# Log-decays summed by two f16 products instead of one f32 product, from the eleventh attention tile on

## The chip, the cores and the metric

The kernel runs on one core of a Trainium2 chip. The time is that of one launch in device microseconds (us). Below, PE is the matrix engine (TensorE), with PEld its loads of stationary operands; DVE is the vector engine, ACT the scalar engine, POOL the GpSimd engine; SP issues the transfers (DMA).

## The reference

A gated linear attention over 4 batches, 8 heads, 768 steps and 48 features a head is followed by a two-layer network over 3072 tokens and by a network of eight experts of 384 tokens each. What the change touches is the attention's decay:

```python
f = 1.0 / (1.0 + np.exp(-f_logit))
for t in range(S):
    state = f[:, :, t, :, None] * state + np.einsum('bhd,bhe->bhde', k[:, :, t], v[:, :, t])
    y[:, :, t] = np.einsum('bhd,bhde->bhe', q[:, :, t], state)
x = np.maximum(0.01 * (x @ w_in), x @ w_in) @ w_out     # then the experts: relu(x @ w1[e]) @ w2[e]
```

## The kernel before

The attention is cut into 24 tiles, numbered 0 to 23: 128 steps of one batch, all eight heads. Inside a tile the decay between two steps is a difference of running sums of log f. So each tile begins with these sums (`s0`, line 394): ACT forms exp(-f_logit) in place in `fT` (three buffers), then log(1 + that) into `ld` (two buffers, 64 columns a head, of which 48 hold data and 16 stay zero); PE multiplies `ld` by `span`, a 128x128 matrix of 0, 1 and -1, one f32 product for each of the four pairs of heads, into the PSUM tile `P`. One f32 product stands in the trace as two weight loads and two matmuls.

`s1` takes the exponentials of P and -P on ACT (`ek`, `eq`, and `dn` for the next state) and multiplies them onto k and q on DVE (`ks`, `qs`), and decays the state (`de`, `St`). `s2` transposes `ks` (`kT`, `kp`). `s3` forms the products A of `ks` and `qs`, which DVE masks (`am`); from tile 8 on `am` is split into high and low f16 halves (`ahl`, ACT and DVE). `s4` forms the output `y` and the state's update `U`; `ys` is y in two f16 halves, which `s5` turns with a transposing DMA into `xT`.

The two-layer network runs on PE beside the attention, three tiles of tokens at a time (a group). Its operands are f16 halves too: `hp` (first layer, 16 blocks a group, three PSUM buffers) is turned by ACT and DVE into `g`, and `g` is split into `gh` (ACT) and `gl` (DVE, in some early blocks POOL); `xp` is the second layer. The weights of both layers arrive as pairs of 32-bit words and are put together by DVE integer operations (`winu`, `woutu`), then split (`winh`, `winl`, `wo`). DVE does this up to the last `wo`, which the first `xp` reads in order of its index f, 0 to 15. After that the experts' weights are loaded (`xw_s`), split (`xw_h` on ACT, `xw_l` on DVE) and stored; `pg` are small products for the later routing, on operands that a transposing DMA delivers (`turned`).

The order of the instructions on each engine is set when the program is built: the first tiles by hand (`START`), the rest by a scheduler, which interleaves the attention's steps with the network's products. Nearly all instructions are recorded by one helper, so they bear the line 84.

Of the kernel before, what the change touches and what calls it, by code (L numbers as in the profile page):

```python
# [10 lines left out]
F16 = mybir.dt.float16  # L11
# [3 lines left out]
AF = mybir.ActivationFunctionType  # L15
OP = mybir.AluOpType
# [2 lines left out]


SQ, SV = 64.0, 64.0
SX, SWI, SG, SWO = 2.0 ** 10, 2.0 ** 7, 2.0 ** 10, 2.0 ** 8
SWG = 2.0 ** 12
SX2, SW1, SW2 = 2.0 ** 6, 2.0 ** 8, 2.0 ** 8
# [67 lines left out]
def body(tc, qk, v, f_logit, w_in, w_out, w_gate, w1, w2, out):  # L92
    nc = tc.nc
    w_in, w_out = w_in.bitcast(I32), w_out.bitcast(I32)
    PE, DVE, ACT, POOL, SP = (InOrder(tc, e) for e in (nc.tensor, nc.vector, nc.scalar, nc.gpsimd, nc.sync))
    InOrder.on = True
    B, CH, _, D, _, NP, _ = qk.shape
    H, S = 2 * NP, 128 * CH
# [9 lines left out]
    NWD = 0  # L108
    NWARM, WU = 0, 4
    MP = (1,)  # L110
    LEAD, PACE0, W0, POOLN, GLN, FT, KP, PB = 3, 1300.0, 1000.0, 8, 2, 8, 4, 3

    with ExitStack() as ctx:
        consts = ctx.enter_context(tc.tile_pool(name="consts", bufs=1))
# [15 lines left out]
        def mm(o, l, r, start, stop):  # L130
            return PE.matmul(o, l, r, start=start, stop=stop, skip_group_check=True)

        def copy(o, i, scale=1.0):
            return ACT.activation(o, i, AF.Copy, bias=0.0, scale=scale)
# [82 lines left out]
        one = consts.tile([128, 1], F32)  # L217
# [11 lines left out]
        dnext = [[apool.tile([128, NP], F32, name=f"dn{b}_{i}") for i in range(2)] for b in range(B)]  # L229
# [7 lines left out]
        span = consts.tile([128, 128], F32)  # L237
# [3 lines left out]
        DVE.tensor_scalar(early, late, -1.0, None, op0=OP.add)  # L241
        DVE.tensor_scalar(span[:, :MID + 1], jp[:, :MID + 1], 0.0, early, op0=OP.is_le, op1=OP.mult)
        DVE.tensor_scalar(span[:, MID + 1:], jp[:, MID + 1:], 0.0, late, op0=OP.is_ge, op1=OP.mult)
        identf = consts.tile([128, 128], F32)
        DVE.tensor_scalar(identf, jp, 0.0, None, op0=OP.is_equal)
        identh = consts.tile([128, 128], F16)
# [147 lines left out]
        def s0(n):  # L394


            t, u = XT["f", n], ld[n % 2]
            ACT.activation(t, t, AF.Exp, bias=0.0, scale=-1.0)
            ACT.activation(u[:, :, :D], t, AF.Ln, bias=one, scale=1.0)
            yield  # L400
            P = banks[0].tile([128, NP, 128], F32, name="P", tag="at", bufs=5)
            for p in range(NP):
                mm(P[:, p, :], u[:, 2 * p:2 * p + 2, :], span, True, True)
            st.setdefault(n, {})["P"] = P


# [12 lines left out]
        def s1(n):  # L419

            c, b = tiles[n]
            P = st[n].pop("P")
            ek, eq = edec[0][n % 2], edec[1][n % 2]
            qs = aw.tile([128, NP, 128], F32, name="qs")
            ks = aw.tile([128, NP, 128], F32, name="ks")
            for t, sign in ((ek, 1.0), (eq, -1.0)):
                ACT.activation(t[:, :, :MID + 1], P[:, :, :MID + 1], AF.Exp, bias=0.0, scale=sign)
                ACT.activation(t[:, :, MID + 2:129], P[:, :, MID + 1:], AF.Exp, bias=0.0, scale=sign)
            if c + 1 < CH:
                ACT.activation(dnext[b][c % 2], P[:, :, 127], AF.Exp, bias=0.0, scale=-1.0)  # L430
            yield
            (POOL if n < KP else DVE).tensor_tensor(ks, XT["qk", n][:, 1], ek[:, :, 1:129], op=OP.mult)
            DVE.scalar_tensor_tensor(qs, XT["qk", n][:, 0], SQ, eq[:, :, 1:129], op0=OP.mult, op1=OP.mult)
            st[n].update(qs=qs, ks=ks)
            if c > 0:
                de = aw.tile([128, NP], F32, name="de")
                DVE.tensor_tensor(de, dnext[b][(c - 1) % 2], ek[:, :, 0], op=OP.mult)
                DVE.tensor_tensor(St[b], St[b], de[:, :, None].to_broadcast([128, NP, 2 * D]), op=OP.mult)
# [631 lines left out]
        n = 0  # L1070
# [12 lines left out]

        live, complete = {}, set()
        names = dict(f=s0, v=s0v, p=s1, k=s2, a=s3, y=s4, x=s5, w=split_win)

        def group_x(n):
# [242 lines left out]
```

## Time and profile before

| | |
|---|---|
| time, median of 3 runs | 785.66 us (784.7 to 787.34) |
| the profiled execution | 781.42 us, of which the span of its instructions is 779.6 us |
| mean granted clock of TensorE | 0.983 of 2.4 GHz |
| PE busy | 94% of the span |
| DVE busy | 72% of the span, 99% of it between 40 and 156 us |
| products P of tiles 10 to 23 | start at 118.51 to 358.98 us |

The profiled execution lies 4.2 us under the median of the three runs, so rows of the trace are summed against 781.42 us, and the difference is carried over to the median. Busy time on PE is modelled at the ends of matmuls, which overlap in the pipeline: how long a group of products holds PE is read from the starts of what stands before and behind it.

### The profile page before, as it was taken

Reading aid. Unit: us, or ns where it says so; the run is one execution under the profiler, and the core shown is the slowest. Engines: PE = TensorE matmul, PEld = TensorE weight load, DVE = VectorE, ACT = ScalarE, POOL = GpSimd, SP = SyncE. Lnnn points to the kernel's source line nnn. Section 1 sums busy time; section 2 is a strip of 40 time slices with the busy share of each in tenths; the row PEclk is TensorE's granted clock in tenths of the full one; section 3 lists DMA queues with packets and bytes.
Section 4 is the critical chain, followed back from the end, with each engine's and each line's share of the span. In section 5 each row is a group of like instructions: output and inputs, shape, how many; then the busy total and the mean of one; then the engine's idle time right before and its main releaser. Section 6 shows DMA issues by size and latency. Waiting matters only on the chain.

```text
span 779.6 us, 15455 instructions
## 1 busy us (share of the span) xinstructions
PE 730.7 (94%) x5900; PEld 484.1 (62%) x5900; DVE 558.8 (72%) x1579; ACT 350.0 (45%) x732; POOL 142.7 (18%) x158
## 2 busy tenths in 40 slices
PE   6888998999999999998999999999989899999995
PEld 5756775677576577676666666555545455556663
DVE  5899999968966967966873958677685676873320
ACT  6566656557755754753663743000123123222320
POOL 5355312000000000000000001010243434535111
PEclk9899899999999999999999999999999999999998
DMA  9965544698897798998898500050475557665300
GB/s 258 249 162 164 161 133 125 152 276 219 237 249 213 210 309 191 250 249 221 238 272 230 166 2 2 23 192 22 148 224 155 177 158 168 228 198 174 107 31 30
DMA packets 111643, 135.90 MB, mean 174 GB/s; under 512 B 62929, under 2 KB 94674, under 8 KB 109522
## 3 DMA queue, kind: packets, MB, share of 16 engines
q1 hardware_dynamic: 106194, 100.31, 49.1%
q0 software_dynamic: 5376, 34.61, 13.1%
q8 instruction: 46, 0.75, 0.4%
q14 instruction: 27, 0.22, 0.1%
HBM read 86.52 MB, written 34.60 MB: 155 GB/s over the span
## 4 chain that ended last, share of the span: by engine, by line
PE 49%; DVE 25%; DMA 9%; issue 8%; ACT 5%; SPq 1%; POOL 1%; another core or an unknown queue 1%; POOLq 0%; ACTq 0%; DVEq 0%
PE hp L84 17%; PE xp L84 17%; PE yp L84 5%; DVE g L84 3%; PE y L84 3%; DVE winu L84 3%; DMA xw_s<-in_moe_w 3%; DMA fT<-in_f_logit 2%; DVE gl L84 2%; DVE woutu L84 2%; DMA turned<-x 2%; DVE xw_l L84 1%; PE P L84 1%; PE U L84 1%; PE c L84 1%
## 5 line engine op out<-in xcount | busy, mean ns | idle before, releaser
L84 PE MATMUL hp<-xT,winh 128*128 128x384 f16 x768 | 191.4, 329 | 11.8 <-DVE g L84 11.7
L84 PE MATMUL xp<-wo,gh 128*128 128x384 f16 x768 | 190.4, 326 | 0.8 <-DVE wo L84 0.8
L84 PE MATMUL hp<-xT,winl 128*128 128x384 f16 x384 | 126.3, 329 | 0.0
L84 PE MATMUL xp<-wo,gl 128*128 128x384 f16 x384 | 125.0, 326 | 0.0
L84 PEld LDWEIGHTS <-gh 128*128 128x128 f16 x912 | 83.9, 97 | 42.6
L84 PEld LDWEIGHTS <-winh 128*128 128x128 f16 x768 | 74.3, 99 | 57.3 <-issue 16.5
L84 PE MATMUL hp<-x2T,w1e 128*128 128x384 f16 x576 | 99.3, 325 | 0.7 <-ACT x2T L84 0.4
L84 PE MATMUL yp<-w2e,hh 128*128 128x384 f16 x384 | 94.4, 325 | 0.0
L84 ACT ACTIVATE g<-hp 128x384 f32<-128x384 f32 x152 | 73.0, 485 | 23.1 <-PE hp L84 21.5
L84 DVE SCALAR_TENSOR_TENSOR g<-hp,g 128x384 f32<-128x384 f32 x128 | 69.5, 552 | 8.2 <-ACT g L84 7.8
L84 PEld LDWEIGHTS <-w1e 128*128 128x128 f16 x576 | 52.3, 97 | 32.9 <-issue 1.1
L84 PEld LDWEIGHTS <-gl 128*128 128x128 f16 x528 | 48.7, 97 | 28.6 <-DVE gl L84 0.9
L84 ACT ACTIVATE gh<-g 128x768 f16<-128x768 f32 x64 | 53.9, 841 | 26.1 <-DVE g L84 25.4
L84 ACT ACTIVATE xw_h<-xw_s 128x768 f16<-128x768 f32 x64 | 53.2, 839 | 25.5 <-DMA xw_s<-in_moe_w 24.7
L84 POOL IOTA jp<- 128x128 f32 x2 | 0.5, 238 | 341.8 <-PE hp L84 341.7
L84 PE MATMUL yp<-w2e,hl 128*128 128x384 f16 x192 | 62.5, 325 | 0.0
L84 DVE TENSOR_TENSOR gl<-g,gh 128x768 f16<-128x768 f32 x52 | 49.7, 956 | 16.8 <-ACT gh L84 16.2
L84 DVE SCALAR_TENSOR_TENSOR xw_l<-xw_s,xw_h 128x768 f16<-128x768 f32 x64 | 60.2, 951 | 1.9 <-ACT xw_h L84 1.9
L84 ACT ACTIVATE hh<-hp 128x384 f16<-128x384 f32 x64 | 31.4, 491 | 62.2 <-PE hp L84 52.1
L84 ACT ACTIVATE x<-yp 128x384 f32<-128x384 f32 x24 | 11.8, 491 | 93.3 <-PE yp L84 75.1
L84 ACT ACTIVATE x<-xp 128x384 f16<-128x384 f32 x24 | 11.7, 489 | 92.0 <-PE xp L84 80.8
L84 PEld LDWEIGHTS <-winl 128*128 128x128 f16 x384 | 37.8, 98 | 22.9 <-issue 0.9
(265 smaller groups left out, 1228.3 us busy)
## 6 DMA issues: line engine op xcount, KB each, us to landing
xw_s<-in_moe_w SPq DMA_DIRECT2D x64, 384.0 KB, 4.0
qkT<-in_qk SPq DMA_DIRECT2D x48, 192.0 KB, 4.1
wout_s<-in_moe_w_out SPq DMA_DIRECT2D x16, 384.0 KB, 3.5
w1d<-xw_h SPq DMA_DIRECT2D x32, 192.0 KB, 4.2
w1d<-xw_l SPq DMA_DIRECT2D x32, 192.0 KB, 4.0
w2d<-xw_h SPq DMA_DIRECT2D x32, 192.0 KB, 4.3
w2d<-xw_l SPq DMA_DIRECT2D x32, 192.0 KB, 4.0
fT<-in_f_logit SPq DMA_DIRECT2D x24, 192.0 KB, 3.5
```

The lines of the kernel that those rows point to most:

```text
L84: i = f(*args, **kwargs)
```

## The change

For tiles 0 to 9 nothing changes. From tile 10 on (`HT`), ACT writes the logarithm in place in f32, ACT copies it, scaled by 2^9, as f16 into the first half of the same `ld` buffer, and DVE writes the rest (the scaled value minus that copy) as f16 into the second half. PE sums both halves in PSUM: two f16 products by `spanh`, an f16 copy of `span`, for each pair of heads. The exponentials take the scale out again. The zero columns of the two buffers are cleared once more, in tiles 10 and 11.

```diff
+        spanh = consts.tile([128, 128], F16)
+        DVE.tensor_copy(spanh, span)
...
             ACT.activation(t, t, AF.Exp, bias=0.0, scale=-1.0)
-            ACT.activation(u[:, :, :D], t, AF.Ln, bias=one, scale=1.0)
+            if n < HT:
+                ACT.activation(u[:, :, :D], t, AF.Ln, bias=one, scale=1.0)
+            else:
+                u = u.rearrange("p h d -> p (h d)").bitcast(F16).rearrange("p (s h d) -> p s h d", s=2, h=H)
+                if n < HT + 2:
+                    DVE.memset(u[:, :, :, D:], 0.0)
+                ACT.activation(t, t, AF.Ln, bias=one, scale=1.0)
+                copy(u[:, 0, :, :D], t, SLD)
+                DVE.scalar_tensor_tensor(u[:, 1, :, :D], t, SLD, u[:, 0, :, :D], op0=OP.mult, op1=OP.subtract)
...
-                mm(P[:, p, :], u[:, 2 * p:2 * p + 2, :], span, True, True)
+                if n < HT:
+                    mm(P[:, p, :], u[:, 2 * p:2 * p + 2, :], span, True, True)
+                else:
+                    for i in range(2):
+                        mm(P[:, p, :], u[:, i, 2 * p:2 * p + 2, :], spanh, i == 0, i == 1)
...
-            for t, sign in ((ek, 1.0), (eq, -1.0)):
+            a = 1.0 if n < HT else 1.0 / SLD
+            for t, sign in ((ek, a), (eq, -a)):
```

The scheduler also places other instructions anew. Three places matter here. The first is DVE where it prepares the last `wo` blocks (about 121 to 128 us of the trace); `g` is the evicted first layer. Before:

```order
L84 TENSOR_SCALAR woutu<-wout_s 128x384
L84 SCALAR_TENSOR_TENSOR g_1305<-hp,g_1305 128x384
L84 SCALAR_TENSOR_TENSOR woutu<-wout_s,woutu 128x384 x2
L84 TENSOR_TENSOR de<-dn_1_126,ek_109 128x4
L84 SCALAR_TENSOR_TENSOR woutu<-wout_s,woutu 128x384
L84 TENSOR_TENSOR am<-A,mask 128x512 x2
L84 SCALAR_TENSOR_TENSOR wo<-woutu,wo 128x384
L84 SCALAR_TENSOR_TENSOR g_1305<-hp,g_1305 128x384
```

The same place on DVE after the change (the first and the second `g` row are the same two blocks, under new numbers):

```order
L85 SCALAR_TENSOR_TENSOR woutu<-wout_s,woutu 128x384 x2
L85 SCALAR_TENSOR_TENSOR g_1307<-hp,g_1307 128x384
L85 SCALAR_TENSOR_TENSOR woutu<-wout_s,woutu 128x384 x2
L85 TENSOR_SCALAR woutu<-wout_s 128x384
L85 TENSOR_TENSOR am<-A,mask 128x512 x2
L85 SCALAR_TENSOR_TENSOR wo<-woutu,wo 128x384
L85 SCALAR_TENSOR_TENSOR g_1307<-hp,g_1307 128x384
```

Counted from the program's start to the second `g` row, one `wo`, two `woutu` and one `de` now stand behind it, and one `memset` and one low half (both tile 10's, some rows earlier) ahead of it.

The second place is PE at P of tile 12, beside the first tile of the second layer (`xp`). Before:

```order
L84 MATMUL xp<-wo,gh 128x384
L84 LDWEIGHTS gh
L84 MATMUL xp<-wo,gh 128x384
L84 MATMUL P<-span,ld_105 128x128 x4
L84 MATMUL A<-qs,ks 128x128 x8
L84 LDWEIGHTS gl
L84 MATMUL xp<-wo,gl 128x384
```

The same place on PE after the change, where six more P rows, an `xp` row among them and the last two A follow the last row shown:

```order
L85 MATMUL P<-spanh,ld_105 128x128
L85 LDWEIGHTS gh
L85 MATMUL xp<-wo,gh 128x384
L85 LDWEIGHTS gl
L85 MATMUL xp<-wo,gl 128x384
L85 MATMUL A<-qs,ks 128x128 x5
L85 LDWEIGHTS gh
L85 MATMUL xp<-wo,gh 128x384
L85 MATMUL A<-qs,ks 128x128
L85 LDWEIGHTS ld_105
L85 MATMUL P<-spanh,ld_105 128x128
```

The high half's first product now goes ahead, and the rest, which needs the low half, stands behind six of A's products; the low half of block f = 15 is read only behind 26 other products of `xp`.

The third place is DVE at about 194 to 200 us, as it stands in the ten or so tiles that follow. Before:

```order
L84 SCALAR_TENSOR_TENSOR g_2264<-hp,g_2264 128x384
L84 SCALAR_TENSOR_TENSOR xw_l<-xw_s,xw_h 128x768
L84 TENSOR_TENSOR de<-dn_0_127,ek_110 128x4
L84 TENSOR_TENSOR St_120<-St_120,de 128x384
L84 TENSOR_TENSOR am<-A,mask 128x512 x2
L84 SCALAR_TENSOR_TENSOR g_2264<-hp,g_2264 128x384
L84 TENSOR_TENSOR ahl<-am,ahl 128x512 x2
L84 TENSOR_TENSOR gl<-g_2264,gh 128x768
L84 SCALAR_TENSOR_TENSOR g_2326<-hp,g_2326 128x384 x2
L84 SCALAR_TENSOR_TENSOR xw_l<-xw_s,xw_h 128x768
```

The same place on DVE after the change:

```order
L85 SCALAR_TENSOR_TENSOR g_2298<-hp,g_2298 128x384
L85 SCALAR_TENSOR_TENSOR xw_l<-xw_s,xw_h 128x768
L85 TENSOR_TENSOR de<-dn_0_127,ek_110 128x4
L85 SCALAR_TENSOR_TENSOR ld_106<-fT_104,ld_106 128x8x48
L85 TENSOR_TENSOR am<-A,mask 128x512 x2
L85 SCALAR_TENSOR_TENSOR g_2298<-hp,g_2298 128x384
L85 TENSOR_TENSOR ahl<-am,ahl 128x512 x2
L85 TENSOR_TENSOR gl<-g_2298,gh 128x768
L85 SCALAR_TENSOR_TENSOR g_2366<-hp,g_2366 128x384 x2
L85 SCALAR_TENSOR_TENSOR xw_l<-xw_s,xw_h 128x768
L85 TENSOR_TENSOR St_120<-St_120,de 128x384
```

The low half takes the place of the state's decay (`St`), which moves behind the next `xw_l`.

## Rows read from the trace of the kernel before

**Rows 1.** Windows: busy us of PE, PEld, DVE, ACT, POOL, clock, DMA share.
```profile
108.00:156.00 48.00, 43.98 (x356) 31.63 (x356) 47.42 (x93) 28.65 (x63) 5.71 (x3) 0.96 0.52 136
156.00:360.00 204.00, 199.70 (x1731) 139.53 (x1728) 154.25 (x277) 124.86 (x251) 0.00 (x0) 1.00 0.91 240
```
**Rows 2.** Waits of DVE, 40 to 156 us: total us, times, longest.
```profile
DVE g L84 <- ACT g L84: 0.2, 1, 0.2
```
**Rows 3.** Waits of PE, 108 to 156 us.
```profile
PE hp L84 <- DVE g L84: 3.4, 3, 2.1
PE xp L84 <- DVE wo L84: 0.8, 2, 0.6
```
**Rows 4.** Waits of PE, 156 to 360 us.
```profile
PE hp L84 <- DVE g L84: 2.6, 4, 0.9
PE pg L84 <- DMA turned<-wo: 1.6, 1, 1.6
```
**Rows 5.** Timeline of PE about P of tile 13: start, us, merged count.
```profile
161.07 1.05 PE L84 MATMUL P<-span,ld 128*128 128x128 f32 x8
162.06 1.16 PE L84 MATMUL A<-qs,ks 64*128 64x128 f32 x16
```
**Rows 6.** Timeline of PE, f16 products of P's size late in the program.
```profile
557.26 0.78 PE L84 MATMUL xT<-identh,xg 128*128 128x128 f16 x11
```
**Rows 7.** Timeline of PE, from an f16 product to A.
```profile
405.61 0.33 PE L84 MATMUL xp<-wo,gh 128*128 128x384 f16 x1
405.86 1.16 PE L84 MATMUL A<-qs,ks 64*128 64x128 f32 x16
```
**Rows 8.** Tile views (`ld`, `xT`): ns min/median/max, first and last start.
```profile
L84 PE MATMUL P<-span,ld x192: 271/275/582, 5.3 to 359.8; 128*128 128x128 f32 x192
...
L84 DVE MEMSET ld<- x2: 165/165/165, 3.4 to 3.5; 128x128 f32 x2
...
L84 PE MATMUL xT<-identh,xg x54: 216/219/230, 557.3 to 736.3; 128*128 128x128 f16 x54
```
**Rows 9.** Groups by form: busy us, mean ns, idle before.
```profile
L84 DVE SCALAR_TENSOR_TENSOR vl<-ld_v,vh 128x384 f16<-128x384 f32 x16 | 8.8, 549 | 0.0
...
L84 ACT ACTIVATE vh<-ld_v 128x384 f16<-128x384 f32 x16 | 8.4, 522 | 0.0
L84 PEld LDWEIGHTS <-xg 128*128 128x128 f16 x54 | 3.3, 98 | 1.3 <-DMA xg<-x2d,row 1.0
```
**Rows 10.** Timeline of DVE: four operations in a row; the state's decay.
```profile
139.34 1.96 DVE L84 SCALAR_TENSOR_TENSOR woutu<-wout_s,woutu 128x384 int32<-128x384 int32 x4
...
151.11 0.55 DVE L84 TENSOR_TENSOR St<-St,de 128x384 f32<-128x384 f32 x1
```
**Rows 11.** Timeline, DVE and PE: the longest wait of PE after 108 us.
```profile
127.04 0.56 DVE L84 SCALAR_TENSOR_TENSOR g<-hp,g 128x384 f32<-128x384 f32 x1
...
127.65 0.48 PE L84 MATMUL hp<-xT,winh 128*128 128x384 f16 x2 [2.14 <-DVE g L84]
...
130.20 0.84 PE L84 MATMUL hp<-xT,winh 128*128 128x384 f16 x2
```
**Rows 12.** Timeline, DVE and PE: the last `wo` and its reader.
```profile
150.10 0.55 DVE L84 SCALAR_TENSOR_TENSOR wo<-woutu,wo 128x384 f16<-128x384 f32 x1
...
150.74 0.49 PE L84 MATMUL xp<-wo,gh 128*128 128x384 f16 x2
```
**Rows 13.** Timeline of PE: P of tile 15 and a wait behind it.
```profile
190.59 1.05 PE L84 MATMUL P<-span,ld 128*128 128x128 f32 x8
...
199.60 0.48 PE L84 MATMUL hp<-xT,winh 128*128 128x384 f16 x2 [0.92 <-DVE g L84]
```
**Rows 14.** Timeline of PE: P of tile 23 and the wait behind it.
```profile
358.98 1.05 PE L84 MATMUL P<-span,ld 128*128 128x128 f32 x8
...
367.37 0.30 PE L84 MATMUL pg<-wgs,turned 128*128 128x16 f16 x6 [0.47 <-DMA turned<-wo]
```

More of the change, by code (lines that the diff above doesn't have):

```diff
@@ L21 @@
 SQ, SV = 64.0, 64.0
+SLD = 2.0 ** 9
 SX, SWI, SG, SWO = 2.0 ** 10, 2.0 ** 7, 2.0 ** 10, 2.0 ** 8
@@ L110, in body @@
     MP = (1,)
-    LEAD, PACE0, W0, POOLN, GLN, FT, KP, PB = 3, 1300.0, 1000.0, 8, 2, 8, 4, 3
+    LEAD, PACE0, W0, POOLN, GLN, FT, KP, PB, HT = 3, 1300.0, 1000.0, 8, 2, 8, 4, 3, 10
     with ExitStack() as ctx:
@@ L429, in s1 @@
             if c + 1 < CH:
-                ACT.activation(dnext[b][c % 2], P[:, :, 127], AF.Exp, bias=0.0, scale=-1.0)
+                ACT.activation(dnext[b][c % 2], P[:, :, 127], AF.Exp, bias=0.0, scale=-a)
             yield
```

## The prediction

> **What bounds the kernel now.** I read the busy time by windows first, then who waits for whom in each window, then single places. The windows [rows 1] split the stretch in which tiles 10 to 23 form their sums into two stages. From 108 to 156 us DVE is busy 47.42 of 48.00 us. In the view of DVE's waits [rows 2] only 0.2 us stand in front of it between 40 and 156 us: DVE is full, and PE, which waits 3.4 us for `g` and 0.8 us for `wo` there [rows 3], follows it. From 156 to 360 us it is the other way round: PE is busy 199.70 of 204.00 us and DVE 154.25, and PE's waits for DVE come to 2.6 us [rows 4]. So a microsecond taken off PE is worth a microsecond in the second stage, and in the first a microsecond put on DVE costs one. Tiles 10, 11 and 12 lie in the first stage, tiles 13 to 23 in the second.
>
> **PE, removed and added.** P of tile 13 starts at 161.07 and A behind it at 162.06 [rows 5]: the four f32 products hold PE for 0.99 us. Inside, eight matmuls start (1.05 - 0.275)/7 = 0.111 us apart (0.275 is how long one lasts [rows 8], 1.05 the row's length); the last is followed by A only 0.99 - 0.775 = 0.215 later, some 0.10 more than the spacing. After the change there are eight f16 products of 128 columns, each with weights of its own. The nearest rows are the f16 products `xT`, of the same size and with new weights nearly each time: eleven in 0.78 us [rows 6], one of 0.219 [rows 8], so (0.78 - 0.219)/10 = 0.056 apart. The step into A costs something too: an `xp` product of the usual 0.16 us is followed by A after 405.86 - 405.61 = 0.25 [rows 7], 0.09 more. I take 7 x 0.056 + 0.056 + 0.09 = 0.54 us, so a saving of 0.99 - 0.54 = 0.45 us a tile; with a step of 0.215 it is 0.38, with none 0.54. Those are the bounds.
>
> **DVE, added.** One low half a tile: the same operation on the same size as `vl`, 0.549 us [rows 9]. Back to back such operations overlap: four in 1.96 us [rows 10] are (1.96 - 0.55)/3 = 0.47 apart. I take 0.47, with 0.55 as the bound. Two clearings, of 0.165 each by the like one at the start [rows 8]. The f16 copy of `span` comes once, at the very start, where DVE next waits for PE and ACT to deliver the first tile; nothing, and at most the 0.55 of one of DVE's usual operations.
>
> **ACT, added.** One f16 copy a tile, 0.522 us like `vh` [rows 9]. ACT is busy 124.86 of 204 us in the second stage [rows 1], and eleven copies add 5.7. The copy stands ahead of `ek` in most tiles, so `ks` and `qs` come half a microsecond later; the A that reads them stands a tile behind, and the network's products between cover it; without that cover it would be 0.5 us a tile. Nothing. The input buffer `fT` is now let go by DVE's low half, so its next load starts up to about 1 us later (a copy and a low half); loads run two tiles ahead, which covers that too.
>
> **The first stage, up to about 156 us.** By the order, the second `g` row of the first place loses a `wo`, two `woutu` and a `de` ahead of it (3 x 0.47 + 0.1 = 1.5 us) and gains a clearing and a low half (0.165 + 0.47 = 0.64). PE waits 2.14 us for exactly this row at 127.65 [rows 11]; the wait should shrink by about 0.9. But the work is only put off. Up to the last `wo`, and to the first `xw_l` behind it, DVE does two clearings and four low halves more (2 x 0.165 + 4 x 0.47 = 2.2 us), less a `de` and an `St` that move behind (about 0.6, from the 0.55 of rows 10): 1.6 us later if DVE stays full. PE stood directly behind DVE there: the last `wo` ends at 150.65, its reader starts at 150.74 [rows 12]. In the new order PE has 26 other products of `xp` (26 x 0.16 = 4.2 us) to do ahead of that reader, and three cheaper P (3 x 0.45 = 1.35 us). Tile 12's P, though, waits in its middle for a low half that DVE reaches only after `ys`: a stall of 0 to 1.7 us. These pull both ways; I take the stage as unchanged, with -1.5 and +1.6 us as ends.
>
> **The second stage.** Eleven tiles save 0.45 us each on PE: 4.95. Three of them give nothing, since PE runs into a wait behind them anyway: tile 15's (190.59), with the wait of 0.92 us for `g` at 199.60 [rows 13], tile 18's, which repeats that pattern, and tile 23's (358.98), ahead of the wait for a transposed operand at 367.37 [rows 14]. Eight are left: 8 x 0.45 = 3.6. DVE's added low halves cost nothing while DVE has 50 us of slack in 204; in the tight place (third place of the order) the low half takes the room of an `St` that moves behind, so `g` isn't later. The sum is -3.6 us: 781.42 - 3.6 = 777.8 for an execution like the profiled one, and 785.66 - 3.6 = **782.1** for the median, which lies 4.2 us higher. That is 0.46% faster; 0.3%, some 2.4 us, is about what a measurement here can tell from no change.
>
> **The rivals.**
> *More than forecast.* The first stage shrinks as well. The stretch behind the wait of 2.14 us runs at half the clock: two products of `hp` last 0.84 us at 130.20 where they take 0.48 at 127.65 [rows 11], that is, 1.2 instead of 2.4 GHz, after PE had stood still. With a shorter wait the drop may not come; the granted clock of the stage, 0.96 over 48 us [rows 1], makes it worth (1 - 0.96) x 48 = 1.9 us. 3.6 + 1.5 + 1.9 = 7.0: 778.7. Against it: clearings and low halves keep DVE full, and the wait shrinks by less than half.
> *Nothing gained in sum.* DVE's 1.6 us go through in full and tile 12's stall with them: -3.6 + 1.6 = -2.0, 783.7. For it: DVE has no idle time there at all.
> *The weight loads show.* A load of 128 f16 columns lasts 0.098 us [rows 9]; if it is not hidden behind the product ahead, the eight are 0.098 apart: 7 x 0.098 + 0.19 = 0.88, a saving of 0.11, 8 x 0.11 = 0.9 us, 784.8. The 0.056 of rows 6 speaks against it, there with the same loads. The Trainium skill ("TensorE: Matmul & The Clock Gate", Back-to-back issue gap) gives about 81 ns for each product of 128 columns in a stream of weight loads and products; by it the saving would be 0.99 - (8 x 0.081 + 0.09) = 0.25 a tile, 2.0 in sum, 783.7. This case's row, 0.056, disagrees, and I go by the row.
> *Slower.* DVE becomes the bound in the second stage too: each low half lies on the path. A tile in which it does costs 0.47 us and saves nothing, any other saves 0.45; from six of the eleven on the gain is gone, and with nine it is 9 x 0.47 - 2 x 0.45 = +3.3, 789.0. For it: the four waits for `g`, all where ACT and DVE split the first layer. Against it: DVE's share there rises only to (154.25 + 11 x 0.47)/200 = 80%.
>
> **How the numbers follow.** Forecast (782.1; by the bounds 780.3, with 0.54 in ten tiles, to 782.6, with 0.38 in eight) 0.46; more than forecast 0.15; nothing gained in sum 0.18; the weight loads show 0.04; slower 0.17. The first two are faster by over 0.3%: 0.61. The next two lie within it: 0.22. The last is 0.17. The range is 778.5 to 787.0: it holds all cases but the far half of the first rival and most of the last.
>
> **What would show it.** Right: between P of tiles 13 and later and the A behind them 0.50 to 0.60 us instead of 0.99; PE's waits for `g` from 156 to 360 us near 2.6 to 4; A of tile 22 some 3.5 to 4 us earlier than before; a first `xw_l` between 155 and 158 us. Wrong: products further apart than 0.08; waits for `g` grown by several microseconds in the second stage; PE standing over 2 us in the middle of tile 12's P; a longer stretch at half the clock after 125 us. It would also be wrong if a gain at 360 us were given back to the transposes of the weights that `pg` waits for.

## The result: 0.6% slower, and the profile after

| | before | after |
|---|---|---|
| median of 22 runs each | 784.88 us (779.21 to 791.04) | 789.88 us (785.15 to 794.48) |
| ratio, 95% interval | | 1.0061 (1.0034 to 1.0089) |
| profiled execution; span | 781.42; 779.6 us | 794.37; 792.6 us |

The forecast was 782.1 us and faster; the time lies above the range too. In this ratio and in those below, executions more than 1.5% above the fastest of their kernel are left out (none of the changed kernel's here, two of nine in load_first). The two profiled executions stand 13 us apart because one is among the fastest of its kernel and the other among the slowest. 3.7 us of that lie in the first 66 us, where the work is the same but for the f16 copy of `span` (the ninth `g` row of DVE ends at 66.32 and 70.00 us); in a further profile of the kernel before that row ends at 69.68. So the spans of two profiles can't be compared here. Stretches can, as far as the same kernel repeats them.

The windows of [rows 1], in the changed kernel:

```profile
108.00:156.00 48.00, 42.01 (x343) 30.38 (x339) 46.09 (x91) 28.40 (x63) 5.43 (x3) 0.93 0.50 130
156.00:360.00 204.00, 195.92 (x1698) 133.68 (x1697) 160.44 (x289) 129.77 (x265) 0.00 (x0) 1.00 0.89 238
```

DVE is still nearly full in the first window and has 44 us of slack in the second, and PE is busy 96% of the second where it was 98%. What PE waited for in the second window, with ACT's and DVE's waits that stand behind it (compare [rows 4]):

```profile
ACT fT L85 <- DMA fT<-in_f_logit: 10.3, 6, 4.0
DVE x L85 <- ACT x L85: 8.8, 5, 4.3
PE hp L85 <- DVE g L85: 6.0, 6, 1.8
```

The longest of these waits are one event. The timeline of the changed kernel there, ACT first, then DVE, then PE (in brackets the idle time ahead of the row and who ended it):

```profile
184.82 0.52 ACT L85 ACTIVATE fT<-fT 128x384 f32<-128x384 f32 x1 [4.05 <-DMA fT<-in_f_logit]
185.25 0.47 ACT L85 ACTIVATE x<-xp 128x384 f16<-128x384 f32 x1
...
185.75 0.56 DVE L85 SCALAR_TENSOR_TENSOR x<-xp,x 128x384 f16<-128x384 f32 x1 [4.33 <-ACT x L85]
...
186.37 0.48 PE L85 MATMUL hp<-xT,winh 128*128 128x384 f16 x2 [0.67 <-DVE x L85]
...
189.74 0.48 PE L85 MATMUL hp<-xT,winh 128*128 128x384 f16 x2 [1.75 <-DVE g L85]
...
195.65 0.52 ACT L85 ACTIVATE fT<-fT 128x384 f32<-128x384 f32 x1 [2.30 <-DMA fT<-in_f_logit]
...
196.71 1.02 PE L85 MATMUL U<-ld_v,kp 128*112 128x96 f32 x8 [1.07 <-ACT kp L85]
```

ACT stands for 4.05 us in front of the exponential of tile 16, whose input has not landed. Behind it on ACT wait the evictions of `x` and of three blocks of `g`, though tile 16's P comes only at 228.13 us; PE, short of PSUM buffers, waits for them. A second stand follows, of 2.30 us in front of tile 17's exponential; `kp` is queued behind it, and PE waits 1.07 us for that. From P of tile 14 to P of tile 15 it takes 18.65 us instead of 14.83. The Trainium skill says the same of the queue ("PSUM — Partial Sum Buffer", Engine vs sequencer instructions: the queues of ScalarE, VectorE and GpSimdE are strictly first in, first out), and the trace agrees: x begins at 185.25, as the exponential ends.

Why the input is late, SP's rows for the loads of `fT` of tiles 13 and 16, before:

```profile
93.19 0.39 SPq L84 DMA_DIRECT2D fT<-in_f_logit  x1
...
142.39 0.35 SPq L84 DMA_DIRECT2D fT<-in_f_logit  x1
```

and after, with what stands just ahead of the second:

```profile
113.39 0.33 SPq L85 DMA_DIRECT2D fT<-in_f_logit  x1
...
172.78 0.34 SPq L85 DMA_DIRECT2D x2d<-x  x1
173.17 2.39 SPq L85 DMA_TRANSPOSE turned<-x  x1
...
179.06 0.44 SPq L85 DMA_DIRECT2D ld_v<-in_v  x1
179.59 0.44 SPq L85 DMA_DIRECT2D w1d<-xw_h  x1
180.09 0.43 SPq L85 DMA_DIRECT2D fT<-in_f_logit  x1
```

The load for tile 13 was issued 25 us ahead of tile 10's P and is now issued 11 us ahead of it, because its buffer is let go by a low half that DVE reaches 20.6 us after ACT's copy (112.81 and 92.18). For tile 16 the buffer is free at 163.3 us, but the scheduler, which reckons with the later release, has put the load behind tile 10's transposes, a `turned` operand and stores of expert weights.

In the first window (compare [rows 3, 11, 12]) PE's waits are, in the changed kernel:

```profile
PE xp L85 <- ACT wo L85: 2.9, 1, 2.9
PE hp L85 <- DVE g L85: 2.7, 3, 2.0
```

The wait of 2.14 us for `g` at 127.65 us is gone (the 0.48 at 133.14 is for the next block). But a new one, of 2.03 us and for a block five earlier, stands ahead of tile 10's P, and later on PE stands 2.94 us for a `wo`; about the end of that stand its clock is halved. The timeline of PE, after:

```profile
118.04 0.48 PE L85 MATMUL hp<-xT,winh 128*128 128x384 f16 x2 [2.03 <-DVE g L85]
...
148.77 0.48 PE L85 MATMUL xp<-wo,gh 128*128 128x384 f16 x1 [2.94 <-ACT wo L85]
...
150.59 0.53 PE L85 MATMUL xp<-wo,gh 128*128 128x384 f16 x1
150.91 0.53 PE L85 MATMUL xp<-wo,gl 128*128 128x384 f16 x1
...
153.34 0.53 PE L85 MATMUL xp<-wo,gh 128*128 128x384 f16 x1
153.66 0.53 PE L85 MATMUL xp<-wo,gl 128*128 128x384 f16 x1
```

The window around it (the columns of [rows 1]):

```profile
147.00:156.00 9.00, 7.23 (x56) 5.92 (x55) 7.29 (x18) 2.85 (x6) 0.00 (x0) 0.62 0.24 69
```

Products of `xp` start 0.32 us apart there, and 0.16 at 167 us, that is, at 1.2 instead of 2.4 GHz. The granted clock of 0.62 in 9 us is a loss of (1 - 0.62) x 9 = 3.4 us. The kernel before has its half-clock stretch from 128.9 to 132.3 us, 3.4 us long, which costs 1.7 by the same reckoning. Both are PE's loss, and an upper bound of the kernel's.

What the change was to save did arrive. P and A of tile 13, after (compare [rows 5]):

```profile
167.88 0.61 PE L85 MATMUL P<-spanh,ld 128*128 128x128 f16 x8
168.41 1.16 PE L85 MATMUL A<-qs,ks 64*128 64x128 f32 x16
```

0.53 us instead of 0.99. Where a tile runs from P to P without a wait, it takes 14.24 instead of 14.68 us.

### The profile page after: what moved, and what is told of

It reads as the page before. It is cut to its first block, busy times and chain, and to the rows that moved or that the text cites. A ratio compares the mean times of both kernels' runs of the same rounds, so it can differ in the third digit from the quotient of the medians.

```text
span 792.6 us, 15484 instructions
## 1 busy us (share of the span) xinstructions
PE 737.2 (93%) x5900; PEld 485.3 (61%) x5900; DVE 564.9 (71%) x1596; ACT 355.7 (45%) x746; POOL 141.7 (18%) x158
## 4 chain that ended last, share of the span: by engine, by line
PE 59%; DVE 22%; issue 7%; DMA 5%; ACT 4%; POOL 1%; SPq 0%; another core or an unknown queue 0%; POOLq 0%; ACTq 0%; DVEq 0%
PE hp L85 20%; PE xp L85 19%; PE yp L85 6%; PE y L85 4%; DVE g L85 3%; DMA fT<-in_f_logit 3%; PE A L85 3%; DVE winu L85 2%; PE P L85 2%; DVE woutu L85 2%; PE U L85 2%; DVE gl L85 1%; PE c L85 1%; DMA turned<-x 1%; ACT gh L85 1%
## 5 line engine op out<-in xcount | busy, mean ns | idle before, releaser
L85 PE MATMUL hp<-x2T,w1e 128*128 128x384 f16 x576 | 100.9, 329 | 0.7 <-ACT x2T L85 0.6
```

The source lines that it names most:

```text
L85: i = f(*args, **kwargs)
```

## The experiments

The first theory was that the late loads of `fT` cost the time (**late load**), the rival that DVE's added work does, in the stage in which DVE is full (**DVE's work**). Each kernel was timed beside the kernel before on the same chip. The medians of the kernel before on these chips were 777 to 783 us, so only ratios are compared. Besides, three lengths are taken from each profile, which leave out the spread of the first 95 us. On DVE, (a) is from the end of the 17th `g` row to that of the 4th `x` row, about 95 to 221 us of the span; (b) from there to the 15th `x`, about 221 to 425 us; (c) from P of tile 14 to P of tile 15, a part of (a). Each is the length in one profiled execution; the two profiles of the kernel before differ by 0.3 us in (a) and 1.0 in (b), those of the changed kernel by 0.1 and 3.9. P of tiles 10 to 16 lies in (a), P of tiles 17 to 23 in (b).

| kernel | ratio | 95% interval | (a) us | (b) us | (c) us |
|---|---|---|---|---|---|
| before (profile at hand) | | | 126.03 | 203.64 | 14.83 |
| before_again | 1.0000 | 0.9967 to 1.0032 | 126.34 | 202.61 | 14.83 |
| after (profile at hand) | 1.0061 | 1.0034 to 1.0089 | 132.49 | 202.86 | 18.65 |
| after_again | 1.0079 | 1.0048 to 1.0111 | 132.56 | 198.99 | 19.91 |
| load_first | 1.0037 | 0.9998 to 1.0075 | 128.22 | 200.44 | 14.39 |
| low_first | 0.9980 | 0.9947 to 1.0012 | 129.58 | 199.15 | 15.41 |
| only_10_to_12 | 1.0054 | 1.0023 to 1.0086 | 131.29 | 201.67 | 14.83 |
| low_on_pool | 0.9992 | 0.9961 to 1.0023 | 126.90 | 200.22 | 14.96 |
| from_13 | 0.9997 | 0.9968 to 1.0026 | 126.02 | 200.53 | 14.39 |
| pool_from_13 | 1.0028 | 1.0000 to 1.0057 | 128.55 | 201.79 | 14.71 |
| first_from_13 | 0.9966 | 0.9930 to 1.0002 | 126.49 | 198.28 | 14.39 |
| first_from_13_b | 1.0000 | 0.9966 to 1.0035 | 126.96 | 198.62 | 14.64 |
| f32_copied | 1.0017 | 0.9984 to 1.0049 | 126.19 | 200.58 | 14.83 |
| high_only | 0.9898 | 0.9851 to 0.9944 | 124.34 | 199.29 | 14.38 |

**before_again and after_again** are the two kernels themselves.

> The kernel before, unchanged: its profile on the chip of the other three, and a measure of what a ratio here can tell. Ratio 1.000 within 0.003. The stretch before tile 10's P, which is the same code in all kernels, should come out anywhere from 118 to 125 us, as it did in the profiles so far; from P of tile 13 to P of tile 23 it should take 195 to 198 us.

> The changed kernel, unchanged, beside the variants on one chip. If its loss is in the order of its instructions, all of it comes back: ratio 1.003 to 1.009, tile 14 to 15 18 to 19 us with a wait of ACT for fT of about 4 us, first xw_l 39 to 40 us after P of tile 10. If that wait was an accident of the one profiled execution, it is 0 to 2 us here and the ratio's cause lies elsewhere.

The ratio of 1.000 came with an interval of 0.3% to both sides. The changed kernel lost again what it had lost, with a wait of ACT for `fT` of 4.57 us in the same place: its loss is in the order of its instructions, and most of it in (a), 132.5 against 126.2 us. From P of tile 14 to P of tile 15 it took 19.91 us, more than expected.

**load_first** moves two loads and leaves PE's order as it is.

```diff
-                    SP.dma_start(t, ap(f_logit, ...))
+                    if n in (15, 16):
+                        with tc.high_priority():
+                            SP.dma_start(t, ap(f_logit, ...))
+                    else:
+                        SP.dma_start(t, ap(f_logit, ...))
```

> The changed kernel, with the loads of fT of tiles 15 and 16 given high priority and nothing else: PE's order is word for word that of the changed kernel, SP issues these two loads ahead of other loads, and ACT takes tile 16's exponential and logarithm some 20 us earlier. If the late load is the cause, 3 to 4.5 us less than the changed kernel beside it: ratio to the kernel before 0.999 to 1.003, tile 14 to 15 14.3 to 15 us, waits of PE for g from 156 to 360 us down from 6 to 2 to 4. If DVE's added work up to the first xw_l is the cause, no difference from the changed kernel: 1.004 to 1.008.

Its timeline: ACT takes tile 16's exponential without a wait, and P of tiles 14 and 15 stand 14.39 us apart.

```profile
164.03 0.51 ACT L85 ACTIVATE fT<-fT 128x384 f32<-128x384 f32 x1
...
179.71 0.61 PE L85 MATMUL P<-spanh,ld 128*128 128x128 f16 x8
...
194.10 0.61 PE L85 MATMUL P<-spanh,ld 128*128 128x128 f16 x8
```

PE's waits for `g` from 156 to 360 us fell to 3.3. Beside after_again it gained 1.0079 - 1.0037 = 0.42%, 3.3 us of 783, a little beyond the range in which late load alone would have put the ratio. The two intervals overlap, so the times alone don't show the gain; the profiles do: with the same instructions in the same order on PE, (c) fell by 5.5 us and (a) by 4.3, and 2 us over the kernel before were left. The wait of 2.95 us for `wo` and the half-clock stretch behind it, 6.8 us long, stayed; its 3.4 us less the 1.7 of before would make nearly all of these 2 us. So late load is the larger part, and not all.

**low_first** lets DVE do each low half early, in all fourteen tiles.

```diff
-                copy(u[:, 0, :, :D], t, SLD)
-                DVE.scalar_tensor_tensor(u[:, 1, :, :D], t, SLD, ...)
+                with tc.high_priority():
+                    copy(u[:, 0, :, :D], t, SLD)
+                    DVE.scalar_tensor_tensor(u[:, 1, :, :D], t, SLD, ...)
```

> The copy and the low half are given high priority, so that DVE does each low half soon after its copy and the next load into the same fT buffer starts about as early as before the change; the work is the same. If the late release of fT is the cause (loads of tiles 13 to 16 started a whole tile later, ACT stood 4.05 us in front of one exponential at 184.8 us and let x and g wait), the loss goes: 784.5 to 786, ratio to the kernel before 0.999 to 1.002, no wait of ACT for fT over 2.5 us in 160 to 205 us, and tile 14 to 15 takes about 14.4 us instead of 18.6. If DVE's added work in the first stage is the cause (first xw_l at 39.6 us after P of tile 10 instead of 37.8), nothing changes: 789 to 790, 1.005 to 1.007, or worse, since low halves now go ahead of the work that PE waits for.

The ratio came out where late load wanted it, or below. The profile, of an execution 6 us over the kernel's median, agrees only in part: (c) is down to 15.41 where 14.4 was expected, ACT still stands once for 2.60 us (at 193.19) where late load wanted nothing over 2.5, and 3.4 us over the kernel before are left in (a), with PE's waits for `wo` of 1.44, 0.81 and 2.14 us.

**only_10_to_12** changes the three tiles of the first stage alone.

```diff
-            if n < HT:
+            if not HT <= n < HT + 3:
+                if HT + 3 <= n < HT + 5:
+                    DVE.memset(u[:, :, D:], 0.0)
...
-                if n < HT:
+                if not HT <= n < HT + 3:
...
-            a = 1.0 if n < HT else 1.0 / SLD
+            a = 1.0 if not HT <= n < HT + 3 else 1.0 / SLD
```

> Only tiles 10, 11 and 12 are changed, those in the stage in which DVE is full; two more clearings in tiles 13 and 14 make the zero columns good again. By the order the load of fT of tile 16 stands ahead of the tenth turned output, so ACT should find it in time. DVE's work as a cause of its own: 3 low halves and 4 clearings, 3 x 0.47 + 4 x 0.165 = 2.1 us, and PE's three savings of 0.45 lost behind them: ratio 1.002 to 1.005, and the first layer's block 32 some 2 us later after its block 24 than in the kernel before (63.0 and 63.8 us there). Late load as the only cause: 0.998 to 1.001.

0.54% slower, 5 us more in (a): above what DVE's work was to cost. Block 32 of the first layer comes 69.4 us behind block 24, 5.6 to 6.4 more than in the kernel before, where some 2 were expected. PE's waits from 108 to 170 us:

```profile
PE xp L85 <- ACT wo L85: 5.1, 2, 2.9
```

The place of the second, on ACT's timeline:

```profile
162.14 0.52 ACT L85 ACTIVATE fT<-fT 128x384 f32<-128x384 f32 x1 [2.12 <-DMA fT<-in_f_logit]
162.57 0.51 ACT L85 ACTIVATE wo<-woutu 128x384 f16<-128x384 f32 x1
```

The first wait for `wo` is that of the changed kernel, with the halved clock behind it. The second is late load once more, and for tile 16 again, though the expectation had ACT find that input in time: ACT stands in front of the exponential, and the last `wo` is queued behind it. Its half-clock stretches, 147.0 to 153.8 and 164.1 to 167.5 us, cost (6.8 + 3.4)/2 = 5.1 us, 3.4 more than that of before, and with the 2.1 us of the second wait that is about what (a) lost. So this run doesn't part the two causes cleanly; it shows that a late load costs most where something else is queued behind it on ACT, and that the three tiles of the full stage alone can lose as much as the whole change does.

**from_13, low_on_pool, high_only** each take the low halves away from DVE in the full stage: by starting later (`HT` 13 instead of 10), by giving them to POOL, or by leaving them out.

```diff
 low_on_pool
-                DVE.scalar_tensor_tensor(u[:, 1, :, :D], t, SLD, ...)
+                copy(t, t, SLD)
+                POOL.tensor_tensor(u[:, 1, :, :D], t, u[:, 0, :, :D], op=OP.subtract)
 high_only
-                DVE.scalar_tensor_tensor(u[:, 1, :, :D], t, SLD, ...)
...
-                    for i in range(2):
-                        mm(P[:, p, :], u[:, i, 2 * p:2 * p + 2, :], spanh, i == 0, i == 1)
+                    for i in range(1):
+                        mm(P[:, p, :], u[:, i, 2 * p:2 * p + 2, :], spanh, True, True)
```

> The change begins at tile 13, behind the stage in which DVE is full. If DVE's added work in that stage is the cause, the loss goes and nearly all of the saving stays: 781.5 to 783.5 (0.995 to 0.998). If the late release is the cause, it is only part of the way: fT of tile 16 is still loaded behind the tenth turned output instead of the eighth, so ACT should still stand in front of an exponential for 2 to 4 us between 175 and 190 us: 785 to 789 (1.000 to 1.005).

> The low half goes to POOL (ACT scales the f32 logarithm in place, POOL subtracts the f16 half), so DVE has only the two clearings more; by the order the loads of fT stand where they stood before. Late release and DVE's work both say that the loss goes and PE's saving is left: 780.5 to 783, ratio 0.994 to 0.998, with ACT's one copy more a tile at nothing. If the cause is neither (the f16 products, the clock, ACT's copies), it stays near 789 (1.005); if ACT's two added operations a tile are on the path, 785 to 788.

> The changed kernel without the low halves and their products: P is then the sum of the rounded f16 halves alone. DVE has no low half, ACT's copy lets fT go, PE has four products a tile, 0.99 - (4 x 0.056 + 0.09) = 0.68 us saved. If PE's time is what counts wherever DVE and fT are out of the way: 8 to 11 x 0.68 = 5.4 to 7.5 us, ratio 0.990 to 0.994, P to A 0.30 to 0.35 us. If the stretches in which the first layer's blocks come (after tiles 15, 18, 21) are paced by ACT and DVE whatever PE does: 3 to 4 us, 0.995 to 0.997.

In all three (a) is back at 124.3 to 126.9 us. They take away ACT's long stand together with the low halves, so they show that the loss goes, and not how the two theories share it. In low_on_pool PE still stands 2.74 us for `g` and 2.38 for `wo`, with a half-clock stretch of 3.4 us, and (a) is only 0.7 us over that of the kernel before. In from_13 I was wrong on ACT's wait: the load of tile 16 stands behind tile 10's turned output as I wrote (167.11 us, 25 later than in the kernel before), but close behind it, and ACT never waited over 1.8 us. The ratios of from_13 and low_on_pool are those of no change, though their intervals reach into the ranges of both theories. high_only, in which four products a tile are left, is 1.0% faster, about what PE's time alone would give; DVE's low halves are gone there too. P and A there:

```profile
183.59 0.39 PE L85 MATMUL P<-spanh,ld 128*128 128x128 f16 x4
183.90 1.16 PE L85 MATMUL A<-qs,ks 64*128 64x128 f32 x16
```

**f32_copied** takes the release by DVE alone into the kernel before.

```diff
-            ACT.activation(u[:, :, :D], t, AF.Ln, bias=one, scale=1.0)
+            if n < 10:
+                ACT.activation(u[:, :, :D], t, AF.Ln, bias=one, scale=1.0)
+            else:
+                ACT.activation(t, t, AF.Ln, bias=one, scale=1.0)
+                DVE.tensor_copy(u[:, :, :D], t)
```

> The kernel before with one thing of the change alone: from tile 10 on ACT writes the logarithm in place and DVE copies it to ld, so that fT is let go by DVE; products stay f32, no f16 half, no copy on ACT. Late release: loads of tiles 13 to 16 late again, slower by about what the change lost beside its saving less part of DVE's work, 787.5 to 790 (1.003 to 1.007). DVE's work as the cause: three or four copies of 0.3 to 0.5 us in the full stage, 785.5 to 787 (1.001 to 1.003). Neither: 785 (1.000).

Late load missed here (its range for the ratio began at 1.003, inside the interval), and this narrowed it. The loads of tiles 13 and 14 are nearly as late as in the changed kernel (108.55 and 133.63 us), but that of tile 16 goes out at 166.36, and no exponential waits over 2.0 us. So it isn't enough that DVE lets the buffer go and the load comes late; it costs where ACT comes to the exponential well before its input has landed. PE stood seven times from 125 to 156 us, 5.0 us in all but never more than 1.37 at once, two of its rows:

```profile
129.81 0.48 PE L84 MATMUL hp<-xT,winh 128*128 128x384 f16 x2 [1.26 <-DVE g L84]
...
146.13 0.32 PE L84 MATMUL xp<-wo,gh 128*128 128x384 f16 x1 [1.37 <-DVE wo L84]
```

There is no half-clock stretch behind any of them, and (a) is that of the kernel before.

**pool_from_13, first_from_13** (run twice) put two remedies together: the change from tile 13 on, with the low half on POOL (pool_from_13) or with the priority of low_first (first_from_13).

> Change from tile 13 on, with the low half on POOL: neither DVE nor the loads of fT see it, and the full stage of DVE is left alone. If PE's saving of 0.45 us a tile reaches the end, 8 x 0.45 = 3.6 us: ratio 0.994 to 0.997. If the saving is taken up by waits behind it anyway (the low half on POOL from tile 10 on gave 0.9992), 0.998 to 1.001.

> Change from tile 13 on, and the copy and low half at high priority: the loads of fT stand where they stood before the change, and the full stage of DVE is left alone. If the two causes are all, what is left is PE's saving less what the stretches after tiles 15 and 18 take back: 1.5 to 3 us, ratio 0.996 to 0.998. If the saving doesn't reach the end at all: 0.999 to 1.002.

> The same kernel as first_from_13 on another occasion, since its interval (0.993 to 1.0002) just reaches no change. If stretch by stretch the two causes are all there is: 0.995 to 0.998 again, from the first layer's block 16 to the fourth evicted x within 1 us of the kernel before (126.0 and 126.3 us), and from there to the fifteenth x 2 to 5 us less than before (203.6 and 202.6 us). If the first result was luck: 0.999 to 1.002.

first_from_13 keeps (a) within 1 us of the kernel before and is 4 to 5 us shorter in (b) than the two profiles of it, in both its own, as the last expectation had it. But its ratios were 0.9966 and then 1.0000, where the same expectation had luck; the mean is 0.998. That it beats the kernel before is not shown: single executions spread over 10 to 14 us, and (b) alone differed by 3.9 us in two profiles of the changed kernel. pool_from_13 came out above both of its ranges and is rather slower than faster, with 2.3 us more in (a); why POOL's low half does worse from tile 13 than from tile 10 wasn't tried.

## Why the prediction was wrong, point by point

**PE's saving** was right: 0.53 to 0.54 us from P to A, products (0.61 - 0.22)/7 = 0.056 apart (0.22 is a single one), 0.44 us a tile where nothing waits. By the figure of the Trainium skill that was weighed there ("TensorE: Matmul & The Clock Gate", Back-to-back issue gap: about 81 ns a product) it would be 0.74, an estimate; the trace has 0.53, and the row decides.

**The step that failed first** is the sentence on `fT`: "its next load starts up to about 1 us later (a copy and a low half); loads run two tiles ahead, which covers that too." It took the low half to run as soon as its copy is there. In the stage in which DVE is full, it stands in DVE's queue: the release came 20.6 us behind the copy, the loads a tile later, and for tile 16 the new place on SP cost ACT 4.05 us and PE 3.8 us from tile 14 to 15. load_first shows it: (c) goes from 19.91 to 14.39 us when two loads are moved and PE's order isn't, and 0.42% of the time comes back, as far as the overlapping intervals can tell.

**The step that failed second** is "I take the stage as unchanged". The added DVE work was sized about right: from P of tile 10 to the first `xw_l` it took 37.8 and 39.0 us before and takes 39.6 and 39.9, 1.3 more in the mean against a forecast of 1.6. The wait for that `g` row went altogether, where 0.9 us less was forecast, but the new one of 2.03 us came ahead of it: all waits for `g` from 108 to 156 us fell from 3.4 to 2.7. And the work that was put off was `wo`, and PE then stood for it in one piece, 2.94 us, with the clock halved behind it, at a cost of 3.4 us instead of 1.7 (in the profile of after_again 1.7, as before). The rival "more than forecast" had the mechanism and its place right, a drop of the clock that goes with the long stand, and missed that the stand and the drop would come back twenty microseconds later. That DVE's low halves in this stage are the reason is argued and not shown apart: from_13, low_on_pool and high_only don't have them there and don't lose in (a), but they are rid of ACT's long stand too, and low_on_pool has stands as long. If all that late load leaves is put down to them, they are the smaller cause, 0.9 us of the 6.4 that (a) lost in after_again (with 5.5 of late load, 19.91 - 14.39) and 2.0 in load_first, the difference going with the length of the half-clock stretch. Their cost by themselves isn't settled, since only_10_to_12, which was to give it, ran into a late load of its own. Tile 12's P did not stall: other products filled the 2.8 us in its middle.

**The second stage** was right in sign and too large. In (b) the four profiles with f32 products have 200.6 to 203.6 us, 202.1 in the mean; the nine with high and low f16 products 198.3 to 202.9, 200.1 in the mean: 2.0 us saved, where the seven tiles 17 to 23 less 18 and 23, five at 0.44, would make 2.2. The two groups overlap, and the changed kernel alone has 202.9 and 199.0; its first profile holds another half-clock stretch of 3.4 us, at 376.9. So the agreement is one of means. In (a), behind P of tile 15, some is given back: load_first takes 27.35 us from P of tile 15 to P of tile 16 where the kernel before takes 26.66 and 26.10, with waits for `g` of 1.14, 0.91 and 0.49 us instead of one of 0.9. With the low half on POOL it is 27.66, so DVE's low half isn't what does it there; what does is open. DVE did not become the bound of the whole stage, as the slower rival had it: its low halves cost little from tile 13 on (from_13).

**The signs.** P to A came as forecast. The others came on the wrong side: waits for `g` of 6.0 us from 156 to 360 us (2.6 to 4 forecast), the first `xw_l` at 164.25 us (155 to 158), the longer half-clock stretch; A of tile 22 comes 243.1 us behind P of tile 10, 1.7 later than before and not 3.5 to 4 earlier. From 360 to 480 us `pg` waits 3.0 us for the transposes, 0.8 before (1.9 and 1.0 in the second profiles), though there was no gain at 360 us to give back.

**The sum**: 6.3 us lost in (a), from which PE's savings in seven tiles are already taken off, and 2.0 gained in (b) make 4.3, where the medians say 5.0. The lengths leave two stretches out, and in both the changed kernel is longer. From the ninth to the 17th `g` row it takes 29.7 and 29.8 us (29.6 in load_first) where the kernel before takes 28.8 in both profiles, with a half-clock stretch of 10.2 us instead of 6.8 there. Behind the 15th `x` it takes 357.6 and 357.4 us where the kernel before takes 354.8 and 355.9. No run explains either, so the sum isn't closed.

## What to carry to other kernels

When a buffer is handed from a fast reader to one on a full engine, reckon its release from the queue of that engine, not from the length of the instruction, and follow the load that waits for it into the queue that issues it and to the in-order engine that will stand in front of it. Where an engine is full, work added to it may, as here, come out as one long stand further on; look for what is put off last, and count the clock that can follow. Mean slack over a stage says nothing of a single stand in it: ACT was busy 130 of 204 us here, and its stand of 4.05 us still reached PE.

## What the runs showed of the hardware that was not expected

Between 100 and 205 us of the profiles TensorE's granted clock falls to its lower level (1.2 GHz) only at or right behind a stand of PE (a time in which it stands idle in front of an instruction). Behind 2.94 or 2.95 us (after, load_first, only_10_to_12) it stayed there for 6.8 us, in after_again for 3.4; behind 2.12 to 2.43 us (before, before_again, low_first and seven more) for 3.4. But a stand of 2.74 us (low_on_pool) and those of 2.03 to 2.08 us (six profiles) brought no fall, and one of 1.56 (high_only) did. Seven stands of up to 1.37 us, 5.0 us in all, brought none (f32_copied). So the price of a stand of 2 to 3 us was anything from nothing to another 3.4 us, and the same kernel paid different prices in two executions.

Executions of one kernel spread by 1.5% (779 to 791 us), and the first 66 us, the same work in all profiles but for one small copy, took 66.3 to 73.6 us. A gain or a loss of 2 us is seen in the trace of a stretch long before it is seen in the time.
